# Second MLP layer of a decode block on four column groups, stores of 16 partitions, early loads on two queues

## The chip, the cores and the metric

The kernel runs on one core of one Trainium2 chip. The metric is the device time of a run in microseconds. The profile gives a span, from the first instruction to the last, which is about 1.8 us less than the time of the same run (666.7 and 668.45 us for the kernel before).

## The reference, cut to what matters

A decode step for 8 batches: modulation of a layer norm, grouped-query attention with 8192 cached keys and values for 8 key/value heads, a projection, a second modulated layer norm and an MLP with squared ReLU.

```python
mod = (_silu(c) @ w_mod).reshape(c.shape[0], 6, 1, -1)      # sa, ca, ga, sb, cb, gb
h = _layernorm(x) * (1 + ca) + sa
x = x + ga * attention(h, k_cache, v_cache, wq, wo)         # caches: 8 x 8 x 8192 x 128, twice: 268 MB
h = _layernorm(x) * (1 + cb) + sb
x = x + gb * (relu(h @ w1 + b1) ** 2 @ w2 + b2)             # 512 -> 1792 -> 512
```

Only 8 rows of activations meet 284 MB of weights and caches, so the kernel is a stream of loads with work hidden beneath it.

## The kernel before

Caches come in units of 4 MB into a ring of four slots. The first two key units, the bias rows and the projection weights are all issued on SyncE's queue, behind w_mod and w_q:

```python
load(0); load(1)                       # ring slots 0 and 1, nothing to wait for
dma("sync", s_bb, ... b1_row[0:3] ...); dma("sync", s_bb, ... b1_row[3:4] ...)
d_bb = dma("sync", s_bb, ... b2_row ...)
d_wo = dma("sync", s_wo, ... wo_sb ...)
load(2); load(3)                       # wait for the matmuls that read w_mod and w_q out of slots 2 and 3
```

The end of the kernel: W1 and W2 are loaded into a freed slot behind the last values. W2 comes in four pieces, each with its own semaphore (`d_w2`). The second layer keeps W2 as the weights and streams 8 columns of activations, which gives a transposed result. That result is gated, brought back to rows through an identity matmul that also adds the residual, copied out of PSUM in two halves and stored in two transfers:

```python
for f in range(FT):                                   # FT = 14
    for k in range(KT):                               # KT = 4
        t = matmul(yT_ps[:, k, :], W2v[:, f, k * 128:(k + 1) * 128], hidT[:, f, :], deps=[k_sq[f // 8], d_w2[f // 4]])
... o_ps[64 * cc:64 * cc + B, 128 * k:...] = x1T[:, 2 * cc + k, :] times IDENT       # residual
k_y2 = tensor_tensor(y2T, yT_ps, mod(5), ALU.mult)                                    # gate
for cc in (1, 0):
    ... o_ps[64 * cc:64 * cc + B, ...] += y2T[:, 2 * cc + k, :] times IDENT           # back to rows
    ... copy to out_sb: VectorE for cc = 0, ScalarE for cc = 1
    d_o.append(dma(("sync", "scalar")[cc], s_out[cc], outf[:, 256 * cc:256 * (cc + 1)] <- out_sb[rows, :]))
```

(Calls are shortened here; cuts are marked with dots.)

## Time and profile before

| | before |
|---|---|
| time, median of the first three runs | 668.51 us (668.28 to 668.56) |
| span of the profiled run | 666.7 us |
| TensorE busy, DMA engines busy | 79%, full in 39 of 40 slices |
| rate in the loop (160 to 560 us) | 432 GB/s |
| last W2 semaphore, stores issued, last landing | 663.33, 664.85 and 664.92, 666.27 us |

How to read it: a full DMA row means that neither TensorE nor VectorE can shorten the loop. Only what comes after the last bytes is open. The trace has two records for the end of a transfer: the packet, and the landing, which is the moment the semaphore counts up. The last W2 packet ended at 662.90 us, its landing came at 663.33 us. TensorE waits for the landing: its first matmul on that piece starts at 663.37 us.

### The profile page before, as it was taken

Reading aid. Unit: us, or ns where it says so; the run is one execution under the profiler, and the core shown is the slowest. Engines: PE = TensorE matmul, PEld = TensorE weight load, DVE = VectorE, ACT = ScalarE, POOL = GpSimd, SP = SyncE. Lnnn points to the kernel's source line nnn. Section 1 sums busy time; section 2 is a strip of 40 time slices with the busy share of each in tenths; the row PEclk is TensorE's granted clock in tenths of the full one; section 3 lists DMA queues with packets and bytes.
Section 4 is the critical chain, followed back from the end, with each engine's and each line's share of the span. In section 5 each row is a group of like instructions: output and inputs, shape, how many; then the busy total and the mean of one; then the engine's idle time right before and its main releaser. Section 6 shows DMA issues by size and latency. Waiting matters only on the chain.

```text
span 666.7 us, 15924 instructions
## 1 busy us (share of the span) xinstructions
PE 528.3 (79%) x7259; PEld 352.2 (53%) x7259; DVE 307.9 (46%) x587; ACT 264.3 (40%) x307; POOL 20.5 (3%) x79
## 2 busy tenths in 40 slices
PE   3494976898849987599858988499776998589887
PEld 2383732675328742477316753287424773277535
DVE  1262741466316652367415662167513673146633
ACT  2151631466115651166314661166512663146611
POOL 7400000000000000000000000000000000000000
PEclk9696998799969999699998999799997999879996
DMA  9999999999999999999999999999999999999997
GB/s 375 437 406 441 419 433 433 425 434 431 438 427 433 433 434 427 434 434 425 434 431 438 427 431 434 434 427 431 438 425 434 433 436 427 431 434 434 427 420 285
DMA packets 12189, 283.85 MB, mean 426 GB/s; under 512 B 1261, under 2 KB 1297, under 8 KB 3601
## 3 DMA queue, kind: packets, MB, share of 16 engines
q1 hardware_dynamic: 12128, 283.65, 99.3%
q8 instruction: 9, 0.15, 0.1%
q10 hardware_dynamic: 48, 0.02, 0.0%
q14 instruction: 4, 0.02, 0.0%
HBM read 283.66 MB, written 0.01 MB: 425 GB/s over the span
## 4 chain that ended last, share of the span: by engine, by line
PE 52%; DMA 38%; ACT 6%; DVE 2%; issue 1%; SPq 0%; DVEq 0%
PE PS L488 36%; DMA ring<-in_A_k_cache_dram 33%; PE PS L505 9%; ACT P_sb L582 5%; DMA ring<-in_A_v_cache_dram 4%; DMA ring<-in_A_wq_dram 2%; PE PS L636 2%; PE PS L478 1%; ACT KTb L493 1%; DVE O_sb L656 1%; PE PS L472 1%; PE PS L594 1%; DVE Pm L608 0%; PE PS L614 0%; PE PS L773 0%
## 5 line engine op out<-in xcount | busy, mean ns | idle before, releaser
L488 PE MATMUL PS<-IDENT,ring 128*128 128x128 bf16 x4096 | 267.1, 227 | 56.2 <-DMA ring<-in_A_k_cache_dram 56.2
L488 PEld LDWEIGHTS PS<-IDENT,ring 128*128 128x128 bf16 x4096 | 246.5, 102 | 104.8 <-DMA ring<-in_A_k_cache_dram 57.4
L493 ACT ACTIVATE KTb<-PS 128x1024 bf16<-128x1024 bf16 x192 | 196.5, 1024 | 236.6 <-PE PS L488 236.6
L495 DVE COPY KTb<-PS 128x1024 bf16<-128x1024 bf16 x320 | 210.0, 688 | 146.5 <-PE PS L488 144.4
L636 PE MATMUL PS<-ring,Pm 128*32 128x512 bf16 x1018 | 67.2, 409 | 24.8 <-DMA ring<-in_A_v_cache_dram 23.9
L505 PE MATMUL PS<-KTb,Qb 128*32 128x512 bf16 x1024 | 79.0, 385 | 4.5 <-ACT KTb L493 4.5
L656 DVE CAST O_sb<-PS 128x512 bf16<-128x512 f32 x31 | 21.5, 692 | 112.7 <-PE PS L636 112.7
L636 PEld LDWEIGHTS PS<-ring,Pm 128*32 128x32 bf16 x1018 | 26.5, 101 | 61.8 <-DMA ring<-in_A_v_cache_dram 33.7
L535 ACT ACTIVATE KTb<-PS 32x192 bf16<-32x192 f32 (+1 forms) x18 | 5.6, 310 | 110.0 <-PE PS L472 103.9
L582 ACT ACTIVATE P_sb<-PS,negm 128x1024 bf16<-128x1024 f32 x32 | 35.2, 1111 | 20.2 <-DVE negm L577 20.2
L478 PE MATMUL PS<-ONES 128*128 128x512 f32 x80 | 42.1, 630 | 0.0
L472 PE MATMUL PS<-IDENT 128*128 128x512 bf16 x112 | 33.4, 380 | 0.0
L594 PE MATMUL PS<-IDENT,P_sb 128*128 128x128 bf16 x256 | 19.9, 220 | 15.4 <-ACT P_sb L582 15.4
L608 DVE COPY Pm<-PS 64x512 bf16<-64x512 bf16 x48 | 20.2, 421 | 25.0 <-PE PS L594 24.5
L594 PEld LDWEIGHTS PS<-IDENT,P_sb 128*128 128x128 bf16 x256 | 14.4, 98 | 25.1 <-ACT P_sb L582 25.1
L505 PEld LDWEIGHTS PS<-KTb,Qb 128*32 128x32 bf16 x1024 | 15.4, 94 | 21.0 <-ACT KTb L493 8.5
L512 DVE TENSOR_REDUCE m<-PS 128x1 f32<-128x512 f32 x32 | 22.1, 689 | 6.6 <-PE PS L505 6.6
L660 PEld LDWEIGHTS PS<-SEL,O_sb 128*128 128x128 bf16 x124 | 5.8, 97 | 30.0 <-DVE O_sb L656 30.0
L478 PEld LDWEIGHTS PS<-ONES 128*128 128x128 f32 x80 | 12.7, 190 | 10.6 <-issue 10.6
L660 PE MATMUL PS<-SEL,O_sb 128*128 128x8 bf16 x124 | 7.8, 169 | 12.3 <-DVE O_sb L656 12.0
L472 PEld LDWEIGHTS PS<-IDENT 128*128 128x128 bf16 x112 | 9.9, 104 | 10.1 <-issue 7.2
L543 PE MATMUL PS<-wo_sb,KTb 128*32 128x512 bf16 x192 | 11.8, 380 | 3.3 <-ACT KTb L535 3.3
(134 smaller groups left out, 147.0 us busy)
## 6 DMA issues: line engine op xcount, KB each, us to landing
ring<-in_A_k_cache_dram SPq DMA_DIRECT2D x32, 4096.0 KB, 34.0
ring<-in_A_v_cache_dram SPq DMA_DIRECT2D x31, 4096.0 KB, 27.8
ring<-in_A_wq_dram SPq DMA_DIRECT2D x1, 4096.0 KB, 19.8
wo_sb<-in_A_wo_dram SPq DMA_DIRECT2D x1, 4096.0 KB, 47.3
ring<-in_w_mod_dram SPq DMA_DIRECT2D x1, 3072.0 KB, 10.5
ring<-in_A_v_cache_dram SPq DMA_DIRECT2D x1, 2048.0 KB, 22.5
ring<-in_B_w_dram SPq DMA_DIRECT2D x3, 512.0 KB, 19.2
ring<-in_B_w_dram SPq DMA_DIRECT2D x1, 1344.0 KB, 17.8
```

Of the source, the lines that this page charges most:

```text
L472: ts = [op("tensor", lambda e: e.matmul(bank(at).rearrange("p (a r) -> p a r", a=4), IDENT[:, :], rhs)) for _ in range(n)]
L478: ts = [op("tensor", lambda e: e.matmul(bank(at).rearrange("p (a r) -> p a r", a=4), ONES[:, :], rhs)) for _ in range(n)]
L488: t = op("tensor", lambda e, j=j, i=i: e.matmul(STG[j][:, i, :], src[:, 32 * k + 8 * j + i, :], IDENT[:, :], is_transpose=True), [loaded[n ...
L493: stg_free[j] = op("scalar", lambda e, j=j, dst=dst: e.activation(dst, STG[j], ACT.Copy), [t])
L495: stg_free[j] = op("vector", lambda e, j=j, dst=dst: e.tensor_copy(dst, STG[j]), [t])
L505: t = op("tensor", lambda e, hf=hf, q=q, rhs=rhs: e.matmul(PS[32 * q:32 * (q + 1), k, :], Qb[:, 2 * p + hf, :], rhs, start=(p == 0 and hf ...
L512: return op("vector", lambda e: e.tensor_reduce(m4[:, k:k + 1], bank(k), AX.X, ALU.max), [t])
L582: exps.append(op("scalar", lambda e, k=k: e.activation(P_sb[:, k, :, :, :], bank(k).rearrange("p (i x) -> p i x", i=8).unsqueeze(2).to_bro ...
L594: t = op("tensor", lambda e, k=k, i=i: e.matmul(STG[k][:, i, :], P_sb[:, k, i, :, :].rearrange("p h x -> p (h x)"), IDENT[:, :], is_transp ...
L608: done.append(op("vector", lambda e, dst=dst, frm=frm: e.tensor_copy(dst, frm), [t, k_pm]))
L636: t = op("tensor", lambda e, m=m, cg=cg, p=p, vt=vt, Obank=Obank: e.matmul(Obank[32 * cg:32 * (cg + 1), :], lhs[:, p, 32 * m:32 * m + 32], ...
L656: t = op("vector", lambda e, osb=osb, Obank=Obank: e.tensor_copy(osb, Obank), [t])
```

## The change

The intent: get rid of the return trip through TensorE at the end. W2 is now streamed and the activations are the weights, on four column groups of 32 columns, so the result comes out as rows. The rows of groups 0 and 1 (and of 2 and 3) are placed so that their 8 batches adjoin, 16 partitions in all, and each pair is stored by one transfer. Besides, the first two key units and the biases go to ScalarE's queue, the first layer makes half its outputs before the other half, many constants are made more cheaply, and some copies move from ScalarE to VectorE.

```diff
-        load(0)
-        load(1)
-        dma("sync", s_bb, ...        # three bias loads
+        load(0, "scalar")            # both also wait for the mod matmuls (k_wm)
+        load(1, "scalar")
+        dma("scalar", s_bb, ...      # three bias loads
...
-        for k in range(KT):
-            for f in range(FT):
+        for hh, (fa, fz) in enumerate(((0, 8), (8, FT))):
+            for k in range(KT):
+                for f in range(fa, fz):
...
-                    yT_ps[:, k, :], W2v[:, f, k * 128:(k + 1) * 128], hidT[:, f, :],
+                    y_ps[32 * k:32 * (k + 1), :], rows32(hidw[:, f, :], k), W2v[:, f, k * 128:(k + 1) * 128],
+                    ..., tile_position=(0, 32 * k), ...
...
-        (residual matmuls, gate, four transposing matmuls, two copies)
+        t = op("vector", lambda e: e.tensor_tensor(y_sb, y_ps, mod5[:], ALU.mult), [t])
+        t = op("vector", lambda e: e.tensor_tensor(out_sb, y_sb, x1_sb, ALU.add), [t, k_res])
-            d_o.append(dma(("sync", "scalar")[cc], s_out[cc], ... outf[:, 256 * cc:256 * (cc + 1)], out_sb[rows, :] ...
+        d_o = [dma(eng, s_out[h], lambda e, h=h: e.dma_start(
+            bass.AP(out.tensor, out.offset + 256 * h, [[128, 2], [D, B], [1, 128]]),
+            out_sb[64 * h + 24:64 * h + 40, :]), [t]) for h, eng in enumerate(("sync", "scalar"))]
```

The target of each store is now a pattern of 2 halves, 8 rows, 128 columns. Before it had 8 rows, 256 columns.

## The prediction

> **What bounds the kernel now.** I read the page first, then busy time by stretches, then the packet records of the DMA queues, then the timeline and the chain of waits of the last 15 us. On the page:
>
> ```profile
> span 666.7 us, 15924 instructions
> ...
> PE 528.3 (79%) x7259; PEld 352.2 (53%) x7259; DVE 307.9 (46%) x587; ACT 264.3 (40%) x307; POOL 20.5 (3%) x79
> ...
> DMA  9999999999999999999999999999999999999997
> ...
> HBM read 283.66 MB, written 0.01 MB: 425 GB/s over the span
> ```
>
> No compute engine is full, and the DMA row is full in 39 of 40 slices. The stretches say how full (columns: length, busy time of PE, PEld, DVE, ACT, POOL, then clock, DMA share, GB/s):
>
> ```profile
> 160.00:560.00 400.00, 324.58 (x4433) 214.18 (x4433) 191.17 (x356) 167.14 (x196) 0.00 (x0) 0.94 1.00 432
> ...
> 658.00:660.00 2.00, 1.72 (x44) 1.73 (x45) 0.51 (x3) 0.00 (x0) 0.00 (x0) 0.50 1.02 409
> 660.00:662.00 2.00, 1.00 (x28) 0.91 (x28) 1.20 (x6) 0.27 (x1) 0.00 (x0) 0.50 0.84 329
> 662.00:664.00 2.00, 1.87 (x55) 1.51 (x51) 0.40 (x2) 0.00 (x0) 0.00 (x0) 0.50 0.13 46
> ```
>
> For 400 us the core moves 432 GB/s with DMA share 1.00, and it keeps moving over 400 GB/s until 660 us, long after the last value unit is in: these are the MLP weights. The packet records refine this. A 32 KB packet takes 1.216 us (16 engines x 32,768 / 1.216 = 431 GB/s), so the queues have no gaps. A 4 KB packet takes 0.160 us (410 GB/s). Counting bytes moved against a line of 434.5 GB/s, the core is 2.7 us behind at 4 us, still 2.9 at 28 us, 3.8 at 60 us (three quarters of a microsecond of which come while the 4 KB rows of wo move, 39 to 51 us), and from there only creeps. Nothing but the first 4 us and the small packets loses DMA time. The last packet of W2 lands at 662.90 us; the four pieces of W2 come in at about 659.2, 660.6, 662.4 and 662.9. So the time is: bytes at DMA speed up to 662.9 us, and 3.8 us of what can only come after them.
>
> The wait of the queue on SyncE looks bad at first sight, but it is not loss: it only means that enough is queued.
>
> ```profile
> SPq L369 <- PE PS L505: 334.3, 30, 20.6
> ...
> ring<-in_A_k_cache_dram SPq DMA_DIRECT2D x32, 4096.0 KB, 34.0
> ```
>
> A key unit lands 34 us after its issue, and 4 MB take 9.7 us, so three and a half units are ahead of the DMA engines. The chain of the page names PE 52% only because it follows such waits back; I trust the share of 1.00.
>
> The end, from the timeline (start, length, what):
>
> ```profile
> 661.68 2.06 PE L773 MATMUL PS<-KTb,ring 128*128 128x8 bf16 x56 [1.00 <-DVE KTb L768]
> ...
> 663.78 0.19 DVE L781 TENSOR_TENSOR KTb<-PS,modT 128x32 bf16<-128x32 f32 x1 [1.56 <-PE PS L773]
> ...
> 664.03 0.38 PE L786 MATMUL PS<-IDENT,KTb 128*8 128x128 bf16 x4
> 664.44 0.37 ACT L793 ACTIVATE KTb<-PS 8x256 bf16<-8x256 f32 x1 [3.90 <-PE PS L786]
> 664.49 0.41 DVE L791 CAST KTb<-PS 8x256 bf16<-8x256 f32 x1 [0.51 <-PE PS L786]
> ...
> 664.92 0.31 SPq L794 DMA_DIRECT2D out_dram<-KTb  x1
> ```
>
> The second layer begins at 661.68 because DVE finishes the activation late, not because of W2. It ends at 663.75, then come the gate, four transposing matmuls, the copies, and the stores at 664.92. From there to the end are 1.81 us of store and receipt.
>
> **What the Trainium skill says.** DMA: Bandwidth & Descriptors, section Specifications, gives a fabric ceiling of 435 GB/s; the 432 GB/s of the loop agrees, so there is no more rate to find in the loop. The same page, section Rules for kernel authors, says that spreading DMAs over several issuing engines does not help bandwidth, only the sequencer's issue time; the kernel before issues nearly all from one queue, so its trace cannot test it, but a queue already full agrees. The same page, Specifications, asks for 512 B at least per transfer, as below that the engine reads, modifies and writes; the new stores have 256 B pieces, and no store of that size is in the trace. TensorEngine Tiling (Array Packing), section Restrictions and Gotchas, says that column tiling excludes fast weight load, while section Performance Considerations recommends swapping the streamed and the stationary side, with column tiling, where the streamed side is 64 or less: that is this change. The trace has column groups at L402: at the halved clock, 32 matmuls of 512 columns on four groups took 3.60 us, so 0.45 us for four together; they do run beside each other.
>
> **The change part by part.**
> *Early loads.* k0 and k1 go to ScalarE's queue, held until the mod matmuls have read w_mod (14.8 us). Before, SyncE's queue then still holds w_q (up to 21.1 us) and now wo as well. 11.5 MB are on that queue without any wait, 26 us of work, so the engines do not run dry. w_q then shares with k0 and comes some 3 us later (its 2.7 MB left at 15 us, part of it alternating with k0), k0 lands near 30 to 35 us against 29.4 now. All of that only swaps the order of the same bytes. PE has room for it: it idles from 51 to 61 us in batch 0. Gain or loss at the end: 0; at the most the 0.75 us that the 4 KB packets of wo lose could shrink if they alternate with 32 KB packets. I book 0.1.
> *Constants on POOL, R4 for SEL, DVE copies for ACT copies.* They run before 30 us or in value phases, where PE and DVE wait for DMA. 0 us. The same for permute, now all on DVE with a value pass put before the projection.
> *First layer.* Output halves are the outer loop now. From hb at 658.28: 16 matmuls of 0.0365 us (42 in 1.53) give the variance at 658.87 instead of 659.66; its matmul 0.44, root 0.28 and reciprocal 0.2 with their gaps end at 659.9. The first half is through at 658.28 + 32 x 0.0365 + 0.44 = 659.9; three DVE operations of 0.24 with gaps put the first activation at 660.75 instead of 661.63. The second layer can start about 0.9 us earlier.
> *Second layer.* As many matmuls, 56, streaming 128 columns of W2 against 32 columns of weights. By L402, 128 columns for four groups take about 0.11 us, but the issue of one matmul takes 0.033 to 0.037 us whatever it streams (L773: 2.06/56), and four are 0.14; without fast weight load perhaps 0.19. Now the data rule: piece three of W2 at 662.4, then six f tiles x 0.14 to 0.19 = 0.85 to 1.15, so the layer ends at 663.3 to 663.6 instead of 663.75. The 0.9 us earlier start is mostly eaten by the wait for W2.
> *After it.* Gone: the residual matmuls that stood between (L778), the four transposes 0.38, the copies 0.41, and a crossing to PE and back. Added: a multiply and an add on 128 x 128. DVE took 0.23 us for 64 columns and 0.29 for 128 (L419, L427), so 0.3 each, with gaps 0.65 to the issue of the stores. Before it was 664.92 - 663.75 = 1.17. Gain 0.5. The new residual matmuls and their copy lie in DVE's and PE's waits.
> *Stores.* Two stores of 16 pieces of 256 B in place of 8 of 512 B, both still in parallel: 0 to 0.3 us more for the small writes; I book 0.1.
> Sum: 0.3 (end of the layer) + 0.5 (after it) + 0.1 (start) - 0.1 (stores) = 0.8 us; 668.5 - 0.8 = **667.7 us**.
>
> **Rivals.** (a) The DMA end hides all but the last step: the layer ends no earlier, weight loads without their fast mode cost as much as the start gains, 256 B writes cost 0.3. For it: W2's last packet at 662.90. Then 668.3. (b) The two queues alternate better than one: wo's slow packets are covered, the 0.75 us come back on top: 666.9. Against: packet durations are serial on each engine, and the skill denies it. (c) The early order starves the ring: SyncE's issue of k2 already blocks for 22.6 us in the kernel before because its queue is full, and if that blocks ScalarE's loads as well, k0 comes at 45 to 50 us, PE becomes the late one in batch 0 and the slots come free late, so the DMA queue runs dry for some microseconds: 670 to 673. Against: three units of slack in the ring. (d) A large gain, over 13 us, would need fewer bytes or idle DMA time; there is neither.
>
> **Range and chances.** Repeated runs differ by 0.3 us. Between (a) and (b) with that noise: 666.8 to 668.5. (c) has perhaps 5%, and even it stays within 2% (13.4 us). Faster 0.01, same 0.98, slower 0.01.
>
> **What would show it.** Right: 432 GB/s in the loop as before; the last W2 packet still near 662.9; the second layer starting near 660.8 with a pause in it for W2; two DVE operations of 0.3 us and then stores. Wrong: a last weight packet moved by over 0.5 us (then the early loads did it), a slice under 420 GB/s between 17 and 100 us (rival c), four matmuls of the second layer over 0.2 us, or over 2 us from store to end.

## The result, and the profile after

The changed kernel took 669.27 us (median of 4 runs, 668.98 to 670.68), the kernel before 668.53 us. The ratio is 1.0016, with a 95% interval of 0.9999 to 1.0033. Ratios here are the mean time of one kernel's runs over that of the other's of the same rounds, so not quite the ratio of the medians quoted. By the 2% rule it is the same; it is not the 0.8 us faster that was predicted, and it lies above the range.

The page of the changed kernel:

```profile
span 667.8 us, 15812 instructions
...
DMA  9999999999999999999999999999999999999996
...
q1 hardware_dynamic: 11826, 275.26, 96.2%
q10 hardware_dynamic: 354, 8.41, 3.0%
...
HBM read 283.66 MB, written 0.01 MB: 425 GB/s over the span
```

The second queue (q10) now carries 8.41 MB, the rest is as it was. Busy time by stretches (columns as in the prediction):

```profile
160.00:560.00 400.00, 331.04 (x4454) 215.92 (x4455) 195.83 (x367) 166.34 (x188) 0.00 (x0) 0.93 1.00 432
...
658.00:660.00 2.00, 1.66 (x36) 1.50 (x37) 0.69 (x4) 0.13 (x1) 0.00 (x0) 0.62 1.03 411
660.00:662.00 2.00, 1.75 (x55) 1.39 (x57) 1.58 (x8) 0.14 (x1) 0.00 (x0) 0.50 0.79 313
662.00:664.00 2.00, 1.29 (x40) 0.84 (x40) 0.03 (x1) 0.00 (x0) 0.00 (x0) 0.50 0.16 56
```

The loop is untouched: 432 GB/s. Counted against a line of 434.5 GB/s, as in the prediction, the core is 3.82 us behind at 60 us against 3.78 before, and 8.43 us at 660 us against 8.42. The split of the early loads neither gained nor lost any bandwidth. (One sign that the prediction names for rival (c), a slice under 420 GB/s between 17 and 100 us, does appear on the page after, 416 in the second slice; but the kernel before has one of 406 in the third, so the sign tells nothing.) So the time came from the end:

```profile
661.28 1.31 PE L772 MATMUL PS<-ring,hidw 128*32 128x128 bf16 x32 [0.17 <-DVE hidw L767]
...
661.97 0.35 PEld L772 LDWEIGHTS PS<-ring,hidw 128*32 128x32 bf16 x16 [0.34 <-DMA ring<-in_B_w_dram]
...
663.30 0.94 PE L772 MATMUL PS<-ring,hidw 128*32 128x128 bf16 x24 [0.71 <-DMA ring<-in_B_w_dram]
663.84 0.14 PEld L772 LDWEIGHTS PS<-ring,hidw 128*32 128x32 bf16 x8 [0.19 <-DMA ring<-in_B_w_dram]
664.30 0.29 DVE L776 TENSOR_TENSOR KTb<-PS,mod 128x128 bf16<-128x128 f32 x1 [2.27 <-PE PS L772]
664.63 0.22 DVE L777 TENSOR_TENSOR KTb<-KTb 128x128 bf16<-128x128 bf16 x1
664.88 0.78 SPq L778 DMA_DIRECT2D out_dram<-KTb  x1
664.89 0.75 ACTq L778 DMA_DIRECT2D out_dram<-KTb  x1
```

This is the timeline; the bracket is the idle time before and what ended it. The second layer (PE its matmuls, PEld its weight loads) stops three times for W2: until 661.97 for the second piece, until 663.30 for the third and until 663.84 for the last. Behind the layer there are only two VectorE operations, as planned. And the issue of a store takes 0.78 us, where the line of the kernel before says 0.31.

Split at the last W2 landing, the two ends compare so (us):

| stretch | before | after |
|---|---|---|
| last W2 landing (at) | 663.33 | 663.80 |
| to the end of the second layer | 0.42 | 0.48 |
| to the issue of the first store | 1.10 | 0.60 |
| to the last landing of a store | 1.42 | 2.12 |
| SyncE, from its last wait to its branch, within the rest | 0.06 | 0.41 |
| last store landing to the end of the span | 0.46 | 0.79 |
| **W2 landing to the end, in all** | **3.40** | **3.99** |

The gain of 0.50 us is there. Two losses outweigh it: 0.70 us in the stores and 0.35 us in SyncE's last steps. The fourth difference, 0.47 us in the W2 landing itself, had to be shown to belong to the change or to chance.

### The profile page after: what moved, and what is told of

It reads as the page before. It is cut to its first block, busy times and chain, and to the rows that moved or that the text cites. A ratio compares the mean times of both kernels' runs of the same rounds, so it can differ in the third digit from the quotient of the medians.

```text
span 667.8 us, 15812 instructions
## 1 busy us (share of the span) xinstructions
PE 535.9 (80%) x7247; PEld 354.3 (53%) x7247; DVE 316.1 (47%) x610; ACT 257.7 (39%) x288; POOL 13.7 (2%) x37
## 3 DMA queue, kind: packets, MB, share of 16 engines
q10 hardware_dynamic: 354, 8.41, 3.0%
## 4 chain that ended last, share of the span: by engine, by line
PE 53%; DMA 36%; ACT 7%; DVE 3%; SPq 1%; issue 1%; ACTq 0%
PE PS L484 36%; DMA ring<-in_A_k_cache_dram 32%; PE PS L501 9%; ACT P_sb L576 5%; DMA ring<-in_B_w_dram 3%; PE PS L630 2%; PE PS L474 1%; ACT KTb L489 1%; DMA KTb<-in_A_x_dram 1%; DVE O_sb L651 1%; SPq L677 1%; PE PS L468 1%; PE PS L588 1%; PE PS L395 1%; DVE Pm L602 1%
## 5 line engine op out<-in xcount | busy, mean ns | idle before, releaser
L630 PE MATMUL PS<-ring,Pm 128*32 128x512 bf16 x1018 | 70.4, 417 | 40.1 <-DMA ring<-in_A_v_cache_dram 39.2
L468 PE MATMUL PS<-IDENT 128*128 128x512 bf16 x104 | 31.7, 380 | 0.0
L655 PEld LDWEIGHTS PS<-R,O_sb 128*128 128x128 bf16 x124 | 5.8, 96 | 28.8 <-DVE O_sb L651 28.8
L537 PE MATMUL PS<-wo_sb,KTb 128*32 128x512 bf16 x192 | 19.6, 570 | 0.0
L655 PE MATMUL PS<-R,O_sb 128*128 128x8 bf16 x124 | 7.8, 169 | 12.4 <-DVE O_sb L651 12.0
L531 DVE CAST KTb<-PS 32x192 bf16<-32x192 f32 (+1 forms) x34 | 11.8, 346 | 5.9 <-PE PS L518 5.2
```

Source lines behind the costliest of these rows:

```text
L468: ts = [op("tensor", lambda e: e.matmul(bank(at).rearrange("p (a r) -> p a r", a=4), IDENT[:, :], rhs)) for _ in range(n)]
L630: t = op("tensor", lambda e, m=m, cg=cg, p=p, vt=vt, Obank=Obank: e.matmul(Obank[32 * cg:32 * (cg + 1), :], lhs[:, p, 32 * m:32 * m + 32], ...
```

## The experiments

There are sixteen profiles (the two above and those of fourteen runs; e5 repeats the changed kernel and e11 repeats e4), and the last two columns of this table turn out to be the useful ones: the last W2 landing, T, and the time from T to the end of the span.

| run | times, us (sorted) | T | T to end |
|---|---|---|---|
| before, first profile | 668.28 to 668.56 | 663.33 | 3.40 |
| after, first profile | 668.98, 669.02, 669.52, 670.68 | 663.80 | 3.99 |
| e1 four stores | 668.18, 668.28, 668.43, 668.53, 669.74, 669.89 | 662.97 | 3.27 |
| e2 old loads | 668.19, 668.52, 668.54, 668.61, 669.86, 669.90 | 663.06 | 3.65 |
| e3 before, loads split | 668.73, 668.74, 669.65, 669.70, 670.04 | 664.22 | 3.76 |
| e4 four stores, old loads | 668.14, 668.28, 668.30, 668.32, 668.68 | 663.14 | 3.32 |
| e5 after again | 668.75, 669.07, 669.11, 669.27, 669.34 | 662.94 | 3.99 |
| e6 before, target 2 x 4 rows | 668.23, 668.36, 668.38, 668.55, 668.78, 670.17 | 663.55 | 3.41 |
| e7 e4 with 104 more matmuls | 669.46, 669.47, 669.61, 669.90, 670.52 | 664.32 | 3.32 |
| e8 two groups of 256 | 668.71, 668.80, 668.95, 669.71, 669.82 | 663.22 | 3.64 |
| e9 swapped dimensions | 668.57, 668.67, 668.68, 668.69, 668.70, 670.54 | 663.11 | 3.73 |
| e10 first layer as before | 669.05, 669.24, 669.73, 669.92, 670.68 | 663.29 | 4.03 |
| e11 e4 again | 668.31, 668.33, 668.35, 668.45, 669.81 | 663.18 | 3.32 |
| e12 biases on SyncE | 668.77, 668.86, 668.90, 669.11, 669.16 | 663.48 | 3.68 |
| e13 store of two dimensions | 668.14, 668.25, 668.34, 668.55 | 663.01 | 3.41 |
| e14 before, store of three | 669.49, 669.70, 670.40, 670.58 | 663.68 | 4.17 |

T to the end repeats to 0.01 us for the same kernel (3.99 twice, 3.32 twice). T varies from run to run. The runs of the kernel before show two clusters: of 40 runs 12 lie at 669.38 to 670.43 and 28 at 668.05 to 668.78. So a comparison of five runs cannot settle 0.3 us, but the stretch after T can.

**e1: four stores.**

```diff
-        d_o = [dma(eng, s_out[h], ... AP(out, 256 * h, [[128, 2], [D, B], [1, 128]]), out_sb[64 * h + 24:64 * h + 40, :] ...
+        d_o = [dma(("sync", "scalar")[k // 2], s_out[k // 2], ... outf[:, 128 * k:128 * (k + 1)], out_sb[8 rows of group k, :] ...
```

> The changed kernel with its two stores cut into four, each 8 partitions by 128 columns, two per queue. Theory S: the two stores of 16 partitions have 2 as the slowest dimension of their target pattern, so each runs on 2 DMA engines instead of 8 (the landing records show 2 data landings for each against 8 before); this costs most of the 1.1 us that the end behind the store issue grew (2.92 us against 1.81). Then four stores with 8 landings each and issue 0.3 us each bring that stretch back to about 2.1 us: 0.7 to 0.9 us faster than the changed kernel. Rival: the 256-byte pieces cost it; then the stretch stays at 2.7 to 3.0 us and the time too.

```profile
664.04 0.72 SPq L779 DMA_DIRECT2D out_dram<-KTb  x2
664.05 0.65 ACTq L779 DMA_DIRECT2D out_dram<-KTb  x2
```

This is the end of its timeline: two issues per queue take together what one took. From issue to last landing it was 1.80 us instead of 2.12. The lower cluster lies at 668.18 to 668.53 against 668.75 to 669.34 of e5. T to the end fell from 3.99 to 3.27 us, the size that was expected, but the stores gave only 0.32 us of it. The rest is the time from the last landing to the end, 0.40 us in place of 0.79: SyncE's branch came 0.02 us after the last landing. (0.20 us lie between SyncE's last two steps here, but its own second store landed only at 665.84, just before the branch at 665.86, so these 0.20 us are a wait for data.) Right number, half the reason. The first store of each queue had landed 1.20 and 1.40 us after its issue (the records show 8 landings up to 665.25 and 665.44), against 1.23 and 1.35 us in the kernel before, so no slowness of 256-byte pieces is seen here.

**e2: the early loads as before, in the changed kernel.** The edit puts `load(0)`, `load(1)` and the three bias loads back on SyncE's queue, and the wait for wo back to the fifth unit.

> The changed kernel with k0, k1 and the bias rows back on SyncE's queue in the old order. Theory L: the early split over two queues makes the slowest of the 16 DMA engines lag its siblings more (last landing 1.55 us after the median of the 16 in the loop against 1.11 before), and this lag is carried to the end, so that W2 comes 0.45 us later. Then the lag returns to about 1.1 us, the time falls 0.4 to 0.5 us, and the scatter of the changed kernel's runs (668.98 to 670.68) shrinks to about 0.3 us. Rival: the lag is chance of instruction fetches and small transfers, not of the split: it then stays anywhere in 1.0 to 1.6 us and the time does not follow the edit.

T was 663.06. The lag in the loop (of the sixteen landings of a load, the last one less their median, so how far the slowest DMA engine is behind) was 1.14 us, as forecast, but the scatter did not go: two of six runs were at 669.9. The median, 668.57 us, did fall by about 0.5 us (669.11 in e5), as theory L forecast. That was luck: 0.34 us of it is at the very end, where SyncE went from its last wait to its branch in 0.06 us instead of 0.41, and e3 and e5 show that the split does not make the lag.

**e3: only the split, in the kernel before.** Same edit as in the diff above, with two copies moved from ScalarE to VectorE so that they do not hold up ScalarE's queue.

> The kernel before with only the early loads split over two queues (and the two copies that would hold up ScalarE's queue moved to VectorE). Theory L: lag of the slowest engine near 1.55 us, 0.4 to 0.5 us slower than before, with wider scatter. Rival: no change, within 0.2 us.

The lag in the loop was 0.73 us, smaller than before, not 1.55. Theory L, that the split makes one engine late, falls: over the sixteen profiles the lag is 0.73 to 1.52 us with the split and 0.75 to 1.28 us without, and the changed kernel itself has 1.52 us in its first profile and 0.99 in e5. The rival's "no change, within 0.2 us" did not come about either: the two lower runs, 668.73 and 668.74, lie above the lower cluster of before (668.34 to 668.62), and T to the end grew by 0.36 us, all but 0.01 of it at SyncE's end. SyncE's last step again took 0.41 us. And this profile caught a run of the upper cluster:

```profile
662.44 0.56 PE L773 MATMUL PS<-KTb,ring 128*128 128x8 bf16 x16 [0.18 <-DMA ring<-in_B_w_dram]
...
664.27 0.38 PE L773 MATMUL PS<-KTb,ring 128*128 128x8 bf16 x8 [1.26 <-DMA ring<-in_B_w_dram]
```

TensorE waited 1.26 us for the last piece of W2. Fifteen engines had landed it by 662.94, the sixteenth at 664.22. The packet records show why: a 16 KB packet of an instruction queue (q8) runs from 662.10 to 663.20 us, and one last W2 packet of 2 KB starts at 663.18, right behind it. All kernels have that instruction fetch near 662 us, 1.1 us long. In the kernel before and in the changed kernel no W2 packet starts after the end of that fetch. No profile caught an upper run of these two kernels, so that their upper runs have this cause is likely and not shown.

**e4 and e11: four stores and old loads together.**

> Both edits together: the changed kernel with four stores and the old early loads. Theory S and L: 1.1 to 1.3 us faster than the changed kernel, so 667.9 to 668.2 us, 0.3 to 0.6 us faster than before. If only S holds: about 668.4; if only L: about 668.8.

> The candidate of four stores and old loads once more, to see whether it has a slow cluster and lies below before. Terms from the traces: multiply and add in place of transposes and copies -0.57 us, four stores 1.79 against 1.42 us +0.37, SyncE's end as before: 0.2 us below the lower cluster of before. Slow runs in about a third, as in before.

Medians were 668.30 us (before: 668.62) and 668.35 us (668.65). The ratios are 0.9991 (0.9978 to 1.0004) and 0.9997 (0.9984 to 1.0010). T to the end was 3.32 us both times against 3.40 us before, so by the trace this version is better than the kernel before by 0.08 us; e1, with 3.27 us, is better by 0.13. More than that is not shown, as the intervals contain 1. Of the forecasts for e4, 668.30 us is near "If only S holds: about 668.4", though S is not what the later runs leave standing.

**e5: the changed kernel again.**

> The changed kernel unaltered, to have it beside the same runs of before as the experiments. The first experiments showed two clusters of times in the kernel before itself (seven runs 668.34 to 668.62, four runs 669.42 to 670.0). If the changed kernel's own cost is the two-engine store (2.12 us from issue to last landing against 1.79 with four stores and 1.35 before), its lower cluster lies 0.2 to 0.4 us above that of the four-store kernel, at 668.5 to 669.0, and a second cluster 1.1 to 1.3 us higher. Rival (the early split costs 0.5 us by itself): its lower cluster stays at 669.0 or above.

Its lower cluster lies at 668.75 to 669.34, median 669.11 (before: 668.45, ratio 1.0007, 0.9994 to 1.0020). T was 662.94 here against 663.80 in the first profile, with the same code. So the 0.47 us by which W2 came later in the first comparison was chance; T to the end was 3.99 us again.

**e6: the target of the old stores written as 2 x 4 rows.**

> The kernel before with the same bytes in the same 512-byte pieces from the same partitions, but each store's target written as 2 x 4 rows in place of 8, so that its slowest dimension is 2. Theory S (the slowest dimension sets the number of engines): 2 data landings for each store in place of 8, issue of a store 0.5 us or more instead of 0.31, last landing 0.4 to 0.8 us later after the issue than the 1.35 of before, lower cluster 668.9 to 669.3. Rival (the 256-byte pieces cost it): 8 landings or no later than 1.45 us, time as before.

Inconclusive. The records show 8 landings per store, and 1.42 us as before: the rows of a 2 x 4 pattern follow each other at one distance, so the pattern must have been merged to 8 rows. The rival does not win by this, as the test did not take place.

**e7: moving the instruction fetch.** The e4 kernel with 104 tiny matmuls in TensorE's idle time before w_q.

```diff
+        for _ in range(104):
+            op("tensor", lambda e: e.matmul(bank(3)[:, 0:8], IDENT[:, :], IDENT[:, 0:8]))
```

> The kernel of four stores and old loads with 104 tiny matmuls on TensorE in the idle time before w_q has landed (18.8 to 23 us); the result is unused. Theory F: the slow cluster is an instruction fetch of 16 KB on an instruction queue at about 662.1 us (1.1 us long), which in some runs falls on a DMA engine that still has W2 packets left, as in the profile of the split kernel, where one engine's last W2 packet waited from 662.1 to 663.2. PE runs some 128 matmuls with their weight loads between the fetches at 654.2 and 662.1, so 104 more in front move the fetches to about 24 matmuls later: near 655 and near 663, when W2 is in. Then all runs are in the lower cluster, 668.1 to 668.6. Rival: the fetch does not move or the slow runs stay (two or more of six at 669.4 or more).

It went the other way. The fetch moved only from 662.03 to 662.72 us, and all five runs were late, at 669.46 to 670.52. In its profile the fetch at 654.66 us (1.12 us long) fits: the lag of the slowest engine behind the median went from 0.78 us at the last values to 1.93 us at the first piece of W1 and stayed there to the end. So two profiles, e3 and this one, have one DMA engine that falls back by 1.1 to 1.3 us beside a fetch of 1.1 us, and with the 104 matmuls late runs went from one in ten (e4, e11) to five in five. Which engine serves which fetch is not in the records and stays open.

**e8: two groups of 256 columns.**

> The second layer on two column groups of 256 columns instead of four of 128: 28 matmuls, the rows of a batch's half on 8 partitions, so that two stores of 8 pieces of 512 B are enough; loads in the old order. Estimate: two matmuls of 256 columns at the halved clock 0.22 us against 0.14 for four of 128, so six f tiles after the third W2 piece cost 0.5 us more; multiply and add on 256 columns 0.2 us more; the stores 0.45 us less than four stores. Lower cluster 668.3 to 668.7. With 28 fewer matmuls ahead of the end the fetch at 662.1 should come later or not at all (theory F), so no slow runs.

The multiply began 0.99 us after T (664.21) instead of 0.50, the stores took 1.43 us, T to the end 3.64. The estimate of 0.5 us for the wider matmuls holds. The lower runs, 668.71 to 668.95, lie just above the expected 668.3 to 668.7, and the hoped-for absence of late runs did not come about (two of five).

**e9: the two outer dimensions of the store swapped.** Its output is wrong, which doesn't matter for the time.

```diff
-            bass.AP(out.tensor, out.offset + 256 * h, [[128, 2], [D, B], [1, 128]]),
+            bass.AP(out.tensor, out.offset + 256 * h, [[D, B], [128, 2], [1, 128]]),
```

> The changed kernel with the two outer dimensions of the stores' target swapped (8 rows outside, 2 halves inside). Same 16 partitions, same 256-byte pieces, same two stores; the pieces go to wrong places, so the result is wrong on purpose. Theory S (the slowest dimension of the target, 2 or 8, sets on how many DMA engines a store runs): 8 data landings for each store in place of 2, issue 0.3 to 0.45 us in place of 0.75, last landing 1.4 to 1.5 us after the issue in place of 2.12, lower cluster 0.6 to 0.7 us below the changed kernel's (669.1), at 668.3 to 668.6. Rival (piece size or 16 partitions): landing still 1.8 us or more after the issue. The earlier try to force two engines in the kernel before failed: its 2 x 4 rows had 8 landings as before, so the two dimensions had been merged into one.

```profile
664.19 0.84 SPq L778 DMA_DIRECT2D out_dram<-KTb  x1
664.20 0.78 ACTq L778 DMA_DIRECT2D out_dram<-KTb  x1
```

There were 8 data landings per store, as theory S says, but the issue still took 0.84 us, and the last landing still came 2.12 us after it. The number of engines follows the slowest dimension, yet it is not what costs the time. Theory S falls as the cause. The median, 668.69 us, lies close to the 668.3 to 668.6 that S forecast, but for another reason: T to the end is 3.73 us here and not 3.99 because SyncE's last step began at 666.07, when ScalarE's store had landed, and ran beside the wait for its own, which landed at 666.32.

**e13 and e14: taking the third dimension away, and adding one before.** Both give wrong results on purpose.

```diff
 # e13, in the changed kernel: the same 16 pieces, one behind the other
-            bass.AP(out.tensor, out.offset + 256 * h, [[128, 2], [D, B], [1, 128]]),
+            bass.AP(out.tensor, out.offset + 2048 * h, [[128, 16], [1, 128]]),
 # e14, in the kernel before: 8 rows in the order 0, 2, 4, 6, 1, 3, 5, 7
-                outf[:, 256 * cc:256 * (cc + 1)], out_sb[rows, :]), [t]))
+                bass.AP(out.tensor, out.offset + 256 * cc, [[D, 2], [2 * D, 4], [1, 256]]), out_sb[rows, :]), [t]))
```

> The changed kernel with each store's 16 pieces of 256 B put beside each other in the output (wrong places, wrong on purpose), so that the target is a pattern of two dimensions instead of three; same 16 partitions, same pieces, same two stores. Theory P (the third dimension of the pattern costs the descriptor generation): issue 0.31 us in place of 0.75 to 0.84, the sequencer's own increment about 0.5 us after the issue instead of 1.4, last landing 1.3 to 1.5 us after it, time 0.6 to 0.8 us below the changed kernel. Rival Q (16 partitions or 256-byte pieces in one store cost it): issue and landing stay at 0.75 and 2.1 us.

> The kernel before with each store's 8 rows written in the order 0, 2, 4, 6, 1, 3, 5, 7 (wrong on purpose), so that the target has three dimensions that can't be merged; 8 partitions and pieces of 512 B as before. Theory P: issue 0.6 to 0.8 us in place of 0.31, last landing 1.9 to 2.15 us after the issue in place of 1.42, time 0.5 to 0.8 us above before. Rival Q: 0.31 and 1.42 us as before.

The store issues of e13:

```profile
664.09 0.36 SPq L778 DMA_DIRECT2D out_dram<-KTb  x1
664.10 0.39 ACTq L778 DMA_DIRECT2D out_dram<-KTb  x1
```

and of e14:

```profile
665.21 0.74 ACTq L794 DMA_DIRECT2D out_dram<-KTb  x1
665.28 0.75 SPq L794 DMA_DIRECT2D out_dram<-KTb  x1
```

From issue to last landing it was 1.52 us in e13 (16 landings per store) and 2.18 us in e14 (2 landings per store). Theory P holds both ways: the third dimension of the target costs 0.6 to 0.76 us in these stores, with 16 partitions or with 8, with pieces of 256 B or of 512 B. (The number of landings changes in both runs too, but e9 had 8 of them and 2.12 us.)

The times: the median of e13, 668.29 us, lies 0.8 us below that of e5, at the edge of the forecast, and 0.58 us of it are in T to the end. The times of e14, 669.49 to 670.58, lie further above the kernel before than the forecast 0.5 to 0.8 us; only the 0.77 us of T to the end are explained. The increment that e13's forecast has at 0.5 us can't be seen, as all 16 increments there are landings of data.

In the landing records the first increment of a store (the Trainium skill, DMA: Bandwidth & Descriptors, section "Why a DMA increments its semaphore by 16 and not by 1", ascribes it to the issuing sequencer, which does not wait for data) comes 0.5 us after the issue in the kernel before and 1.4 us after it in e5 and e9. The packet records say it more directly: of the first store on each queue, the first data packet starts 0.78 to 0.90 us after the issue where the target has two dimensions (0.79 and 0.81 in the kernel before, 0.90 and 0.87 in e13) and 1.38 to 1.70 us after it where it has three, while the packets of one store are done 0.09 to 0.15 us after the first one starts in both. So the time is spent before the data moves. And of two such stores issued within 0.01 us of each other, one moves its data 0.27 us after the other (1.38 and 1.65 us in the changed kernel); why was not tried.

It is not a rule for any three dimensions: the source of the load of wo has three, and its issue took 0.40 us in the kernel before. Whether it matters here that the source has two dimensions and the target three was not tried.

**e10: the first layer in its old loop order.**

> The changed kernel with the first MLP layer's loop order of before (k outside). Theory W (the second layer ends when the last W2 semaphore has come, plus 0.4 to 0.5 us, whatever its start): the second layer starts 0.8 to 1.0 us later after the attention, near 661.5, and its end stays 0.4 to 0.6 us after the last W2 landing where that landing is at 663.3 or later; where W2 comes early (near 662.9) it is up to 0.4 us later. Time within 0.3 us of the changed kernel's 669.1. Rival (the earlier start is worth its 0.9 us): 669.7 to 670.0.

```profile
661.61 2.13 PE L773 MATMUL PS<-ring,hidw 128*32 128x128 bf16 x56 [1.00 <-DVE hidw L768]
...
663.79 0.29 DVE L777 TENSOR_TENSOR KTb<-PS,mod 128x128 bf16<-128x128 f32 x1 [1.44 <-PE PS L773]
```

The second layer started at 661.61, which is 7.2 us after the last landing of the values, where e5 needs 6.4 (660.43 less 654.03), yet TensorE again stopped for the last piece (the line left out: its weight loads go on at 663.34), and from T to the issue of the stores it was 1.08 us, as in both profiles of the changed kernel. The last piece of W2 lands 8.91 us after the last values in both e5 and e10, so this is not the luck of one landing: the earlier start is worth nothing. The median, 669.73 us, missed the expected 669.1 and lies in the range of the rival (669.7 to 670.0). Two runs are at 669.05 and 669.24; that the other three belong to the upper cluster is a reading of five scattered runs, so it is the trace that speaks against the rival here, not the time.

**e12: only the biases back on SyncE.**

> The changed kernel with only the three bias loads back on SyncE's queue (k0 and k1 stay on ScalarE's). Theory E: the 0.35 us between SyncE's last wait and its branch (0.41 us in the three traces with all five loads moved, 0.06 in the five with none moved, 0.20 in the one with all five moved and one store more on SyncE) depends on how many instructions SyncE's program has, not on what k0 and k1 do to the bandwidth: with three more instructions the gap falls to 0.06 to 0.2 us, and the lower cluster with it by 0.2 to 0.35 us. Rival: the gap comes of the split of k0 and k1 and stays at 0.41.

SyncE's last step took 0.06 us, with k0 and k1, the first two key units, still on ScalarE's queue, and T to the end fell from 3.99 to 3.68. So the 0.35 us hang on SyncE's program and not on the traffic of k0 and k1. All six traces with 0.41 us (after, e3, e5, e9, e10, e13) are programs with the five early loads moved away and no store added; the one with a store added (e1) has no such pause. The nine profiles with 85 or more SyncE instructions have an 8 KB packet of the instruction queue q14 at 645 to 652 us, near SyncE's last loads; the seven with 82 or 83, e1 among them, have none there. That fits a fetch of SyncE's own instructions, but within the pause itself such a packet starts in e3 alone (667.35), so what SyncE waits for was not shown.

## Why the prediction was wrong

**The bound** was right. The loop is DMA-bound before and after, and the early split changed nothing in it (lag 3.78 and 3.82 us at 60 us; 0 was booked but for 0.1). One reading was loose: after 60 us the lag does not only creep, it grows to 8.42 us by 660 us, more than all before it. The line of 434.5 GB/s is just above what the loop does. And between 39 and 51 us, where the prediction has 0.75 us lost, the packet records give 0.65. Rival (b), better alternation, and rival (c), a starved ring, did not come about.

**The end of the second layer, booked as 0.3 us of gain, gave nothing.** The failed step is the sentence that W2's pieces "come in at about 659.2, 660.6, 662.4 and 662.9". The last of these is the end of a packet. The semaphores came at 660.17, 661.46, 662.69 and 663.33, 0.3 to 1.0 us later, and from the last one the layer needs 0.42 us before and 0.48 us after. Both layers already ended on W2. The 0.9 us of earlier start was real (7.25 us after the last landing of the values before, 6.37 us after the change) and was lost in the wait, as rival (a) has it. The cost of four matmuls was within its estimate: 24 in 0.94 us with a stop in it, so at most 0.16 us for four.

**After the layer, 0.5 us was booked and 0.50 us came.** The step with two VectorE operations is right to 0.1 us.

**The stores, booked as 0.1 us of loss, cost 0.70 us.** This is the term that was mis-sized most. The prediction looked at the size of the pieces, and pieces were not it (e1). It did not look at the shape of the pattern. Its own sign of being wrong, "over 2 us from store to end", was the one that caught it (2.91 us). Another one, a last weight packet moved by over 0.5 us, was nearly met by chance (663.38, 0.48 us later) and would have blamed the early loads wrongly.

**SyncE's last step, 0.35 us, was not in the sum at all.** It came with five instructions taken off SyncE's queue, and went when three of them were put back (e12).

Summing what was measured: -0.50 + 0.06 + 0.70 + 0.35 = +0.61 us, against 0.59 us from T to the end in the two traces (3.99 less 3.40). It is also what separates the medians of the first comparison (0.74 us) and of e5 (0.66 us), up to the chance in T.

**The range was too narrow**, apart from this. "Repeated runs differ by 0.3 us" rested on three runs of the kernel before, all of the lower cluster; later 12 of 40 of its runs lay about 1.35 us higher.

## What to carry to other kernels

Where a kernel ends on a transfer, measure from the last semaphore landing, not from the last packet and not from the start: that stretch repeated to 0.01 us in the same kernel while the whole scattered by more than a microsecond. At the end of a kernel compare the issue time of each store in the timeline: merging stores into a three-dimensional target cost more here than two plain two-dimensional stores one after the other. An earlier start of work whose last operand was still on its way bought nothing.

## What the Trainium skill lacked or had wrong

- DMA: Bandwidth & Descriptors, section "Why a DMA increments its semaphore by 16 and not by 1", says that a transfer runs on the largest number of engines, up to 16, that divides the slowest dimension that is not 1 on both of its sides. The traces agree: 2 data landings for 2 halves outside, 8 for 8 rows outside, 16 for 16. It does not say that this can leave the time unchanged: 2.12 us with 2 engines and with 8 (e5, e9).
- The same page has no cost for the dimensions of a pattern on this chip. The stores with three dimensions in the target took 0.74 to 0.84 us to issue, those with two 0.30 to 0.39 us, their first data packet started 1.38 to 1.70 against 0.78 to 0.90 us after the issue, and in programs with two stores the last landing came 2.12 to 2.18 against 1.42 to 1.52 us after it.
- The same page, section Specifications, asks for 512 B per transfer for full rate. No section says what smaller pieces cost in the landing of one small store. The first stores of e1 (2 KB in pieces of 256 B) landed 1.20 and 1.40 us after their issue, the stores of the kernel before (4 KB in pieces of 512 B) 1.23 and 1.35 us: no cost to be seen at this size.
- Runtime: NRT & Kernel Launch, section "Instruction fetch mechanics", says that instructions are fetched by DMA in blocks of 16 KiB and that the cost is mostly hidden. The blocks are in the traces (1.1 us each). It does not say that a fetch can hold up data: in e3 the last W2 packet starts as one ends, and 1.28 us lie between the last and the last but one landing of W2.
- No page has a figure for the pause of 0.41 us on SyncE between its last wait and its branch, which came and went with the number of its instructions (0.06 us in e12). The section just named speaks of stalls at taken branches, without a time; whether this is one was not shown.
